# Loads in order of need in one queue, statistics of two tiles ahead of normalising, and skip terms ahead of the last back rotation, in a fused state-space and SwiGLU kernel

## The chip, the cores and the metric

The kernel runs on one core of one Trainium2 chip. Its engines run beside each other and wait for one another by semaphores: TensorE (PE in the profile, with PEld for its weight loads), VectorE (DVE), ScalarE (ACT), GpSimd (POOL) and SyncE (SP). SP, ACT and POOL also issue DMAs, each into its own queue. The metric is the device time of one execution in microseconds; a smaller one is better. The time given is the median of several executions.

## What is computed

The input x has 2048 rows of 512 values. Each row is normalised (mean and variance, no scale or shift), and two branches are added to x:

```python
xn = _layernorm(x, axis=-1)
return x + _A_ref(xn, ...) + _B_ref(xn, ...)

# A: a diagonal complex state-space layer
Lam_bar = jnp.exp(dt * Lam)
B_bar = ((Lam_bar - 1.0) / Lam)[:, None] * Bmat
Bu = jnp.einsum("bld,pd->blp", x + 0j, B_bar)
h = Lam_bar[None, :] * h + Bu[:, t, :]          # for t in range(2048)
y = 2.0 * jnp.einsum("blp,dp->bld", hseq, Cmat).real + x * Dskip[None, None, :]

# B: a SwiGLU feed-forward layer, 512 -> 1376 -> 512
return (silu(x @ w_gate) * (x @ w_up)) @ w_down
```

Types are bfloat16 in and out.

## The kernel before

**Tiling.** The 2048 rows are 16 tiles of 128 rows, in 4 chunks of 4 tiles. Normalised rows are transposed into xnT (features on partitions), so that a chunk is 512 columns. The 1376 hidden features are 11 tiles, the last of 96 features with a packing of its own.

**Stages for each chunk.** gateup_tile(c, fi) makes one hidden tile: four matmuls of 512 columns with the gate weights and four with the up weights (line 423), then SiLU and a copy on ACT (lines 437 and 438), and for two tiles together a product on DVE (line 442). bproj_tile (line 348) projects into the state space. The recurrence is made real: rotation() multiplies by cosines and sines (lines 358 to 372), DVE scans run along the 512 columns (line 390), and a second rotation turns back into wt. out_ffn (line 510) and out_ssm (line 520) add both branches into one PSUM tile for each row tile.

**The way to the output.** Chunks 0 to 2: out is first set to x by a DRAM to DRAM copy, then the results of out_ssm (copied by ACT into res, line 526) are added to it by accumulating DMAs that POOL issues (line 527). The skip term, xn times Dskip, is made by skip_op: ACT makes xn again into one of three xr buffers (line 482), DVE multiplies it into xall (line 490), and skip_store adds a whole chunk to out with one accumulating DMA on POOL (line 494). For the last chunk skip_op adds the skip term to x (lines 487 and 488), out_ssm adds the matmul result on DVE (line 523), and SP and ACT store it (line 524); the last row tile goes out in three blocks of 256, 128 and 128 columns.

**The order of the work.** PE's order is written out by hand. DVE's long work is held in a backlog of operations, each with a cost in microseconds and a tag. pump(us) is called with the PE time just issued and adds it to what is owed; operations go out while at least half of the next one's cost is owed. An operation may have a part for ACT that goes out when the operation is among the next three. need(tag) sends out the backlog up to the last operation of that tag. multiply() sends out products, which count against what is owed.

**The head (lines 599 to 660).** The first chunk's tiles come one by one. For each: statistics on DVE (ln_stats, or ln_stats_half for half the columns), ln_rstd_act (Ln and Exp on ACT), normalising on DVE (norm_dve, line 203), four transposes on PE into PSUM (xT_pe, line 215), a copy into xnT on ACT or DVE (lines 219 and 217). head_mm then does the gate and up matmuls of the first three hidden tiles for these 128 columns (line 604), into six PSUM banks that are held until all four tiles are through. There are eight banks. Ahead of the first tile, dummy() keeps PE at work on zeros (line 577).

**Loads.** They are issued at the start on SP and ACT in the order of lines 116 to 142. The gate and up weights come in groups of hidden tiles: 0 and 1, then 2, then 3 to 6, then 7 to 9. SP goes on with rows of chunk 1 and with the transposing loads of B (line 135), then weights of group 3, the rest of B and the last weights; load_late brings the others.

Of the kernel before, what the change touches and what calls it, by code (L numbers as in the profile page):

```python
# [23 lines left out]
def kernel(  # L24
# [17 lines left out]
    nc = tc.nc  # L42
    _, L, D = A_x.shape
    Pst = A_Lambda_re.shape[0]
    F = B_w_gate.shape[1]
    assert L % 512 == 0 and D % 128 == 0 and Pst % 128 == 0 and Pst == D
    CW = 512
# [26 lines left out]
    def bank(shape=(128, CW), dtype=F32):  # L74
        return psum.tile(list(shape), dtype, name="ps")
# [10 lines left out]
    xall = const.tile([128, NT, D], BF16, name="xall")  # L86
    xnT = const.tile([128, KD, L], BF16, name="xnT")

    fgroups = [(0, 2), (2, 3), (3, 7), (7, FT - 1)]
    wg_g, wu_g = [], []  # L90
    for gi, (a, b) in enumerate(fgroups):
        cols = min(F, b * 128) - a * 128
# [12 lines left out]
    def wslice(groups, fi, k):  # L105
        for (a, b), t in zip(fgroups, groups):
            if a <= fi < b:
                return t[:, k, (fi - a) * 128:(fi - a) * 128 + fsz[fi]]


    def load_w1(q, tiles, view, gi):
        a, b = fgroups[gi]
        q.dma_start(out=tiles[gi][:], in_=view[:, :, a * 128:min(F, b * 128)])


    nc.sync.dma_start(out=xall[:, 0, :], in_=x_v[:, 0, :])
    nc.vector.memset(xall[:, 1, 0:2], 0.0)
    nc.scalar.dma_start(out=xall[:, 1, :], in_=x_v[:, 1, :])
    load_w1(nc.sync, wg_g, wg_v, 0)
    load_w1(nc.scalar, wu_g, wu_v, 0)  # L120
    load_w1(nc.sync, wg_g, wg_v, 1)
    load_w1(nc.scalar, wu_g, wu_v, 1)
    nc.sync.dma_start(out=xall[:, 2, :], in_=x_v[:, 2, :])
    nc.scalar.dma_start(out=xall[:, 3, :], in_=x_v[:, 3, :])
    nc.scalar.preload_act_table_set("natural_log_exp_and_others")
    load_w1(nc.sync, wg_g, wg_v, 2)
    load_w1(nc.sync, wu_g, wu_v, 2)
    prm_rows = const.tile([128, 128], BF16, name="prm_rows")
    nc.gpsimd.memset(prm_rows[:], 0.0)
    for i, v in enumerate((A_Lambda_re, A_Lambda_im, A_log_dt)):  # L130
# [2 lines left out]
    for part, src in enumerate((A_B_re, A_B_im)):  # L133
        for k in range(KD):
            nc.sync.dma_start_transpose(out=BT[:, part, k, :], in_=src[:, k * 128:(k + 1) * 128])
        if part == 0:
            load_w1(nc.sync, wg_g, wg_v, 3)
            load_w1(nc.sync, wu_g, wu_v, 3)

    nc.sync.dma_start(out=w_last[:, :, 0:LB], in_=wg_v[:, :, FL + LA:F])  # L140
    nc.sync.dma_start(out=w_last[:, :, LB:LB + LA], in_=wg_v[:, :, FL:FL + LA])
# [40 lines left out]
    def ln_stats_half(n, h):  # L182
        nc.vector.bn_stats(out=stats[:, n, h, :], in_=xall[:, n, h * HW:(h + 1) * HW])  # L183
        if h == 1:
            nc.vector.bn_aggr(out=mv[:, n, :], in_=stats[:, n, :, :])
# [3 lines left out]
    def ln_rstd_act(n):  # L189
        nc.scalar.activation(out=lnv[:, n:n + 1], in_=mv[:, n, 1:2], func=ACT.Ln, bias=eps_t[:])  # L190
        nc.scalar.activation(out=rstd[:, n:n + 1], in_=lnv[:, n:n + 1], func=ACT.Exp, scale=-0.5)
# [9 lines left out]
    def norm_dve(n, lo=0, hi=D):  # L201
        c, i = divmod(n, TPC)
        nc.vector.tensor_scalar(out=xn_tile(c)[:, i, lo:hi], in0=xall[:, n, lo:hi], scalar1=mv[:, n, 0:1],  # L203
                                scalar2=rstd[:, n:n + 1], op0=ALU.subtract, op1=ALU.mult)
# [370 lines left out]
    def dummy(n, cols):  # L575
        for _ in range(n):
            nc.tensor.matmul(warm[:, 0:cols], lhsT=junk[:, 0:128], rhs=junk[:, 0:cols], start=True, stop=True)  # L577
# [18 lines left out]
    H = 3  # L596
    held = []

    def head_mm(fi, i, k0=0, k1=KD):
        if len(held) <= fi:  # L600
            held.append((bank(), bank()))
        for ps, groups in zip(held[fi], (wg_g, wu_g)):
            for k in range(k0, k1):
                nc.tensor.matmul(ps[:, i * 128:(i + 1) * 128], lhsT=wslice(groups, fi, k),  # L604
                                 rhs=xnT[:, k, i * 128:(i + 1) * 128], start=(k == 0), stop=(k == KD - 1))

    HK = KD // 2
    dummy(9, CW)
    ln_stats(0)
    ln_rstd_act(0)  # L610
    ln_stats_half(1, 0)
    norm_dve(0, 0, HW)
    xT_pe(0, 0, HK)
    norm_dve(0, HW, D)
    dummy(3, 128)
    xT_pe(0, HK, KD, on_dve=True)
    ln_stats_half(1, 1)
    ln_rstd_act(1)
    for fi in range(2):
        head_mm(fi, 0, 0, HK)  # L620
    for fi in range(2):
        head_mm(fi, 0, HK, KD)
    norm_dve(1)
    xT_pe(1)
    head_mm(2, 0)
    ln_stats(2)
    ln_rstd_act(2)
    ln_stats_half(3, 0)
    for fi in range(H):
        head_mm(fi, 1)  # L630
    norm_dve(2)
    xT_pe(2)
    ln_stats_half(3, 1)
    ln_rstd_act(3)
    nc.gpsimd.iota(out=jidx[:], pattern=[[1, CW]], base=0, channel_multiplier=0,
                   allow_small_or_imprecise_dtypes=True)
    pp = prm_transpose()
    for fi in range(H):
        head_mm(fi, 2)
    norm_dve(3)  # L640
    xT_pe(3, on_dve=True)
    params_a(pp)
    params_a2()
    params_sin()
# [5 lines left out]
    queue("tables", tables[2:])  # L650
    ln_nb(0, TPC)
    for fi in range(H):
        head_mm(fi, 3)
        gu_out(0, fi, *held[fi])
        pump(GU / 4)
    pump(2.0)
# [77 lines left out]
    out_chunk(0)  # L734
    gateup_chunk(2)
    bproj_chunk(3)
    queue_ssm(3)
    out_chunk(1)
    gateup_chunk(3)
    for n in range(0, NT):  # L740
        queue("skip", [skip_op(n, n >= NT - TPC)])
        if n % TPC == TPC - 1 and n < NT - TPC:
            queue("skip", [(0.0, lambda c=n // TPC: skip_store(c))])
    out_chunk(2)
    need("skip")
    out_chunk(3)
# [30 lines left out]
```

## Time and profile before

| what | value |
|---|---|
| median of 3 runs | 183.76 us (183.74 to 183.78) |
| profiled execution: its own time | 184.05 us |
| profiled execution: span | 182.3 us |
| PE busy | 173.8 us, 95% of the span |
| DVE busy | 156.1 us, 86% |
| ACT busy | 104.9 us, 58% |
| POOL busy | 23.5 us, 13% |
| granted PE clock | 1.0 throughout |
| read from and written to HBM | 8.03 MB and 5.24 MB |

The span runs from the first to the last event that the profiler records in the program; the execution's own time holds a little around it. Rows of a timeline give start and length in microseconds, engine, line of the kernel, operation, what is written and read, the number of instructions put together, and in square brackets how long the engine was idle and what released it. SPq and ACTq are the queues in which an engine issues DMAs; the time there is that of issuing, and a DMA's time to landing is given apart from it. Rows of the chain of waits give start, length, and the engine and line that held up the end. Matmul ends are modelled, so a block of matmuls carries a little time behind its last start.

### The profile page before, as it was taken

How to read it: one execution, taken by the hardware profiler on the slowest of the kernel's cores; microseconds unless marked ns; L12 is line 12 of the kernel's file. 1: busy time of each engine (PE TensorE's matmuls, PEld its weight loads, DVE VectorE, ACT ScalarE, POOL GpSimd, SP SyncE). 2: the span in 40 equal slices, each digit the busy share in tenths (PEclk: the TensorE clock that was granted, in tenths of full speed). 3: DMA queues.
4: the chain of work that ended last, by engine and by line, in shares of the span. 5: the costliest groups of instructions: out<-in, count | busy, mean ns of one | idle time of the engine just before them, and what ended most of it. 6: DMA issues, size and time to landing. Idle time of an engine off the chain costs nothing.

```text
span 182.3 us, 2494 instructions
## 1 busy us (share of the span) xinstructions
PE 173.8 (95%) x907; PEld 83.6 (46%) x923; DVE 156.1 (86%) x251; ACT 104.9 (58%) x189; POOL 23.5 (13%) x30
## 2 busy tenths in 40 slices
PE   7779999999999999999999999999999999999990
PEld 2576444444444444444444444444444444444760
DVE  3648999799999999999999999999999999766051
ACT  3329958798479959122699761024867740697000
POOL 6000300000500000014500000015000000222250
PEclk9999999999999999999999999999999999999999
DMA  6999546995034900001750000007300000097755
GB/s 163 322 273 226 87 87 164 352 185 116 1 58 86 345 4 0 0 4 28 97 107 0 0 0 4 0 0 79 36 0 5 0 0 0 0 143 119 104 101 111
DMA packets 29515, 15.53 MB, mean 85 GB/s; under 512 B 19360, under 2 KB 29440, under 8 KB 29472
## 3 DMA queue, kind: packets, MB, share of 16 engines
q1 hardware_dynamic: 24416, 11.34, 25.8%
q0 software_dynamic: 3456, 3.28, 14.2%
q10 hardware_dynamic: 1632, 0.75, 1.5%
q8 instruction: 7, 0.11, 0.3%
q14 instruction: 4, 0.03, 0.1%
HBM read 8.03 MB, written 5.24 MB: 73 GB/s over the span
## 4 chain that ended last, share of the span: by engine, by line
PE 95%; DVE 1%; ACT 1%; issue 1%
PE ps L423 35%; PE ps L510 21%; PE ps L348 15%; PE ps L520 15%; PE ps L604 2%; PE ps L577 2%; PE ps L449 2%; PE ps L459 1%; PE ps L215 1%; ACT xnT L219 1%; DVE xnT L217 0%; DVE xn L203 0%; DVE stats L183 0%; ACT lnv L190 0%; DVE xall L523 0%
## 5 line engine op out<-in xcount | busy, mean ns | idle before, releaser
L510 PE MATMUL ps<-wd_sb,guT 128*128 128x512 bf16 (+4 forms) x195 | 38.6, 355 | 0.2
L423 PE MATMUL ps<-xnT,wg 128*128 128x512 bf16 x143 | 37.6, 379 | 0.3
L423 PE MATMUL ps<-xnT,wu 128*128 128x512 bf16 x146 | 37.5, 379 | 0.1
L390 DVE TENSOR_TENSOR_SCAN g<-r_t,car,u 128x512 bf16<-128x512 f32 x24 | 28.9, 1265 | 0.0
L520 PE MATMUL ps<-CF,wt 128*128 128x512 bf16 (+2 forms) x140 | 28.1, 355 | 0.2
L348 PE MATMUL ps<-xnT,BT 128*128 128x512 bf16 x126 | 28.2, 379 | 0.1
L510 PEld LDWEIGHTS <-guT 128*128 128x128 bf16 (+1 forms) x198 | 18.5, 98 | 19.9
L437 ACT ACTIVATE guT<-ps 128x512 bf16<-128x512 f32 x40 | 25.1, 628 | 3.0 <-PE ps L423 2.9
L438 ACT CAST u<-ps 128x512 bf16<-128x512 f32 x40 | 24.7, 617 | 3.2 <-PE ps L423 3.2
L423 PEld LDWEIGHTS <-wu 128*128 128x128 bf16 x148 | 14.5, 98 | 17.4
L423 PEld LDWEIGHTS <-wg 128*128 128x128 bf16 x148 | 14.3, 98 | 17.6 <-issue 0.8
L526 ACT CAST res<-ps 128x512 bf16<-128x512 f32 x12 | 6.8, 583 | 23.5 <-PE ps L520 23.5
L520 PEld LDWEIGHTS <-wt 128*128 128x128 bf16 x144 | 13.5, 98 | 14.3
L527 POOL DMA_DIRECT2D out_dram<-res x12 | 10.6, 1040 | 72.7 <-ACT res L526 67.6
L348 PEld LDWEIGHTS <-BT 128*128 128x128 bf16 x128 | 12.5, 98 | 15.1
L350 ACT CAST u<-ps 128x512 bf16<-128x512 f32 x32 | 17.7, 613 | 2.3 <-PE ps L348 2.2
L482 ACT ACTIVATE xr<-xall,nb,rstd 128x512 bf16<-128x512 bf16 x16 | 11.6, 804 | 8.5 <-DVE xall L490 8.5
L442 DVE TENSOR_TENSOR guT<-guT,u 128x1024 bf16<-128x1024 bf16 x20 | 13.6, 682 | 0.0
L195 POOL TENSOR_TENSOR rstd<-ve,neg_half 128x4 f32<-128x4 f32 x3 | 5.3, 1751 | 45.4 <-DVE ve L194 45.4
L179 DVE BATCH_NORM_STATS2 stats<-xall 128x6 f32<-128x512 bf16 x14 | 9.4, 671 | 2.0 <-DMA xall<-in_A_x_dram 2.0
L358 DVE TENSOR_TENSOR pm<-u,c 128x2048 bf16<-128x2048 bf16 x8 | 9.8, 1221 | 1.2 <-ACT c L275 1.1
L208 ACT ACTIVATE xn<-xall,nb,rstd 128x512 bf16<-128x512 bf16 x8 | 6.5, 822 | 6.3 <-DVE nb L198 6.3
(103 smaller groups left out, 170.9 us busy)
## 6 DMA issues: line engine op xcount, KB each, us to landing
out_dram<-in_A_x_dram SPq DMA_DIRECT2D x1, 1536.0 KB, 8.9
out_dram<-res POOLq DMA_DIRECT2D x12, 128.0 KB, 3.2
out_dram<-xall POOLq DMA_DIRECT2D x3, 512.0 KB, 6.0
wd_sb<-in_B_w_down_dram SPq DMA_DIRECT2D x1, 1280.0 KB, 9.9
xall<-in_A_x_dram SPq DMA_DIRECT2D x1, 1024.0 KB, 6.7
wg<-in_B_w_gate_dram SPq DMA_DIRECT2D x1, 512.0 KB, 5.7
wu<-in_B_w_up_dram SPq DMA_DIRECT2D x1, 512.0 KB, 6.8
xall<-in_A_x_dram SPq DMA_DIRECT2D x1, 512.0 KB, 6.7
```

The costliest lines, as they stand in the source:

```text
L348: nc.tensor.matmul(ps[:], lhsT=BT[:, part, k, q * 128:(q + 1) * 128], rhs=xnT[:, k, c * CW:(c + 1) * CW], start=(k == 0), stop=(k == KD - 1))
L350: nc.scalar.copy(out=u_tiles[c][:, part, q, :], in_=ps[:])
L358: V.tensor_tensor(out=t[:], in0=flat(src()[:, i]), in1=flat(tab[:]), op=ALU.mult)
L390: V.tensor_tensor_scan(out=g()[:, part, q, :], data0=r_t[:, q:q + 1].to_broadcast([128, CW]), data1=u_tiles[c][:, part, q, :], initial=ini ...
L423: nc.tensor.matmul(ps[:fs, lo:hi], lhsT=wslice(groups, fi, k), rhs=xnT[:, k, c * CW + lo:c * CW + hi], start=(k == 0), stop=(k == KD - 1))
L437: nc.scalar.activation(out=guT[:fs, fi, :], in_=psg[:fs], func=ACT.Silu)
L438: nc.scalar.copy(out=u_pair[c][:fs, fi % 2, :], in_=psu[:fs])
L442: products.append(lambda: V.tensor_tensor(out=g, in0=g, in1=u, op=ALU.mult))
L482: nc.scalar.activation(out=box["xr"][:], in_=xall[:, n, :], func=ACT.Identity, scale=rstd[:, n:n + 1], bias=nb[:, n:n + 1])
L510: nc.tensor.matmul(o[:], lhsT=gu_tiles[c][:fsz[fi], fi, i * 128:(i + 1) * 128], rhs=wd_sb[:fsz[fi], fi, lo:hi], start=(fi == 0), stop=False)
L520: nc.tensor.matmul(o[:], lhsT=w_tiles[c][:, part, q, i * 128:(i + 1) * 128], rhs=CF[:, part, q, lo:hi], start=False, stop=(part == 1 and q ...
L527: nc.gpsimd.dma_start(out=out_v[:, n, lo:hi], in_=res[:, lo:hi], accum_op=ALU.add)
```

## The change

It has three parts.

- Loads. Hidden tiles 0 to 2 become one weight group, of 384 columns, that is loaded in two halves along the contraction (k 0 and 1, k 2 and 3), for gate and for up. All of these go through SP: rows of tile 0, gate halves, rows of tile 2, up halves, rows of tile 3, then the group of tiles 3 to 6. ACT issues the rows of tile 1 alone, and its table load follows at once.
- Head. Statistics of tile 1 are taken whole, ahead of normalising tile 0. There are ten dummies of 512 columns, not nine. Both half copies of tile 0 are on ACT. The head matmuls go by weight matrix: head_mm takes one of the two weight groups, and a list of hidden tiles, and blocks are cut so that transposes of the next tile stand between the groups of one block.
- Tail. The skip operations and stores of chunks 0 to 2 stand in the backlog between the last chunk's scans and its back rotation. They are queued ahead of out_chunk(1). The skip operations of the last chunk stay behind gateup_chunk(3).

```diff
-    fgroups = [(0, 2), (2, 3), (3, 7), (7, FT - 1)]
+    fgroups = [(0, 3), (3, 7), (7, FT - 1)]
...
+    def load_w1_half(tiles, view, gi, k0, k1):
+        a, b = fgroups[gi]
+        nc.sync.dma_start(out=tiles[gi][:, k0:k1, :], in_=view[:, k0:k1, a * 128:min(F, b * 128)])
+
     nc.sync.dma_start(out=xall[:, 0, :], in_=x_v[:, 0, :])
     nc.vector.memset(xall[:, 1, 0:2], 0.0)
     nc.scalar.dma_start(out=xall[:, 1, :], in_=x_v[:, 1, :])
-    load_w1(nc.sync, wg_g, wg_v, 0)
-    load_w1(nc.scalar, wu_g, wu_v, 0)
+    nc.scalar.preload_act_table_set("natural_log_exp_and_others")
+    load_w1_half(wg_g, wg_v, 0, 0, KD // 2)
+    load_w1_half(wg_g, wg_v, 0, KD // 2, KD)
+    nc.sync.dma_start(out=xall[:, 2, :], in_=x_v[:, 2, :])
+    load_w1_half(wu_g, wu_v, 0, 0, KD // 2)
+    load_w1_half(wu_g, wu_v, 0, KD // 2, KD)
+    nc.sync.dma_start(out=xall[:, 3, :], in_=x_v[:, 3, :])
     load_w1(nc.sync, wg_g, wg_v, 1)
-    load_w1(nc.scalar, wu_g, wu_v, 1)
-    nc.sync.dma_start(out=xall[:, 2, :], in_=x_v[:, 2, :])
-    nc.scalar.dma_start(out=xall[:, 3, :], in_=x_v[:, 3, :])
-    nc.scalar.preload_act_table_set("natural_log_exp_and_others")
-    load_w1(nc.sync, wg_g, wg_v, 2)
-    load_w1(nc.sync, wu_g, wu_v, 2)
+    load_w1(nc.sync, wu_g, wu_v, 1)
...
-    def head_mm(fi, i, k0=0, k1=KD):
-        if len(held) <= fi:
-            held.append((bank(), bank()))
-        for ps, groups in zip(held[fi], (wg_g, wu_g)):
+    def head_mm(i, groups, k0=0, k1=KD, tiles=range(H)):
+        which = 0 if groups is wg_g else 1
+        for fi in tiles:
+            if len(held) <= fi:
+                held.append((bank(), bank()))
             for k in range(k0, k1):
-                nc.tensor.matmul(ps[:, i * 128:(i + 1) * 128], lhsT=wslice(groups, fi, k),
+                nc.tensor.matmul(held[fi][which][:, i * 128:(i + 1) * 128], lhsT=wslice(groups, fi, k),
                                  rhs=xnT[:, k, i * 128:(i + 1) * 128], start=(k == 0), stop=(k == KD - 1))
 
     HK = KD // 2
-    dummy(9, CW)
+    dummy(10, CW)
     ln_stats(0)
     ln_rstd_act(0)
-    ln_stats_half(1, 0)
+    ln_stats(1)
     norm_dve(0, 0, HW)
+    norm_dve(0, HW, D)
+    ln_rstd_act(1)
     xT_pe(0, 0, HK)
-    norm_dve(0, HW, D)
     dummy(3, 128)
-    xT_pe(0, HK, KD, on_dve=True)
-    ln_stats_half(1, 1)
-    ln_rstd_act(1)
-    for fi in range(2):
-        head_mm(fi, 0, 0, HK)
-    for fi in range(2):
-        head_mm(fi, 0, HK, KD)
+    xT_pe(0, HK, KD)
     norm_dve(1)
+    head_mm(0, wg_g, 0, HK)
     xT_pe(1)
-    head_mm(2, 0)
+    head_mm(0, wu_g, 0, HK)
     ln_stats(2)
     ln_rstd_act(2)
-    ln_stats_half(3, 0)
-    for fi in range(H):
-        head_mm(fi, 1)
+    head_mm(0, wg_g, HK, KD)
+    head_mm(0, wu_g, HK, KD)
+    ln_stats(3)
     norm_dve(2)
+    ln_rstd_act(3)
+    head_mm(1, wg_g)
     xT_pe(2)
-    ln_stats_half(3, 1)
-    ln_rstd_act(3)
+    norm_dve(3)
     nc.gpsimd.iota(out=jidx[:], pattern=[[1, CW]], base=0, channel_multiplier=0,
                    allow_small_or_imprecise_dtypes=True)
+    head_mm(1, wu_g)
     pp = prm_transpose()
-    for fi in range(H):
-        head_mm(fi, 2)
-    norm_dve(3)
+    head_mm(2, wg_g)
     xT_pe(3, on_dve=True)
+    head_mm(2, wu_g)
     params_a(pp)
...
     for fi in range(H):
-        head_mm(fi, 3)
+        head_mm(3, wg_g, tiles=[fi])
+        head_mm(3, wu_g, tiles=[fi])
         gu_out(0, fi, *held[fi])
...
-    queue_ssm(3)
+    fwd3, back3 = ssm_ops(3)
+    queue("ssm3", fwd3)
+    for n in range(0, NT - TPC):
+        queue("skip", [skip_op(n, False)])
+        if n % TPC == TPC - 1:
+            queue("skip", [(0.0, lambda c=n // TPC: skip_store(c))])
+    queue("ssm3", back3)
     out_chunk(1)
     gateup_chunk(3)
-    for n in range(0, NT):
-        queue("skip", [skip_op(n, n >= NT - TPC)])
-        if n % TPC == TPC - 1 and n < NT - TPC:
-            queue("skip", [(0.0, lambda c=n // TPC: skip_store(c))])
+    for n in range(NT - TPC, NT):
+        queue("skip", [skip_op(n, True)])
     out_chunk(2)
```

The later calls of load_w1 take the new group numbers.

More of the change, by code (lines that the diff above doesn't have):

```diff
@@ L136 @@
         if part == 0:
-            load_w1(nc.sync, wg_g, wg_v, 3)
-            load_w1(nc.sync, wu_g, wu_v, 3)
+            load_w1(nc.sync, wg_g, wg_v, 2)
+            load_w1(nc.sync, wu_g, wu_v, 2)
     nc.sync.dma_start(out=w_last[:, :, 0:LB], in_=wg_v[:, :, FL + LA:F])
```

## The prediction, made before the changed kernel was run

> **What bounds the kernel now.** I read the page first: its span, and the chain of waits by engine.
>
> ```profile
> span 182.3 us, 2494 instructions
> ...
> PE 95%; DVE 1%; ACT 1%; issue 1%
> ```
>
> TensorE (PE) sets the end almost alone. Only time in which PE waits, or time before and after its work, can be won. The stage table (stretch, length, then busy time of PE, PEld, DVE, ACT, POOL, then granted clock, DMA share, GB/s) says where that is:
>
> ```profile
> 5.17:15.03 9.86, 7.58 (x117) 6.92 (x117) 5.32 (x21) 3.87 (x12) 0.00 (x0) 1.00 1.09 288
> 15.03:178.17 163.14, 162.25 (x785) 75.52 (x798) 148.53 (x223) 99.22 (x175) 20.29 (x19) 1.00 0.37 69
> ```
>
> From 15.03 us to the last matmul PE lacks 0.89 us in 163. In the head, 5.17 to 15.03, it lacks 2.28 us by busy time, and more by work: the chain of waits in order of time gives the price of a block.
>
> ```profile
> 9.06 1.50 PE ps L604 x24
> 10.56 0.24 PE ps L215 x4
> 10.80 0.02 issue
> 10.82 0.59 ACT xnT L219
> ...
> 13.22 0.43 DVE xnT L217
> 13.65 0.04 issue
> 13.69 1.50 PE ps L604 x24
> ```
>
> 24 head matmuls (L604) are one column block: 1.50 us with the 0.16 us that the last one drains, so 1.34 us of PE, 0.056 each. Four transposes (L215) cost 0.24. Four blocks and their transposes are 4 x 1.58 = 6.3 us; the stage has 9.86. So about 3.5 us of the head are waiting, and the pattern is in the rows: transposes, then a copy (0.59 on ACT, 0.43 on DVE) while PE has nothing, then 24 matmuls. The first blocks wait longer, for the statistics:
>
> ```profile
> 4.61 0.63 PE L577 MATMUL ps<-junk 128*128 128x512 bf16 x1
> 5.17 0.40 PE L215 MATMUL ps<-ident,xn 128*128 128x128 bf16 x2
> ...
> 7.99 0.40 PE L215 MATMUL ps<-ident,xn 128*128 128x128 bf16 x4 [0.91 <-DVE xn L203]
> ```
> ```profile
> 3.17 0.69 DVE L179 BATCH_NORM_STATS2 stats<-xall 128x6 f32<-128x512 bf16 x1 [1.98 <-DMA xall<-in_A_x_dram]
> ...
> 4.00 0.39 DVE L183 BATCH_NORM_STATS2 stats<-xall 128x6 f32<-128x256 bf16 x1
> 4.77 0.60 DVE L203 TENSOR_SCALAR xn<-xall,mv,rstd 128x256 bf16<-128x256 bf16 x2 [0.38 <-ACT rstd L191]
> ...
> 7.52 0.41 DVE L203 TENSOR_SCALAR xn<-xall,mv,rstd 128x512 bf16<-128x512 bf16 x1 [0.60 <-ACT rstd L191]
> ```
> ```profile
> 4.21 0.29 ACT L190 ACTIVATE lnv<-mv,eps_t 128x1 f32<-128x1 f32 x1
> ...
> 5.60 0.37 ACT L219 COPY xnT<-ps 128x256 bf16<-128x256 bf16 x1 [0.87 <-PE ps L215]
> ```
>
> Units that I take from these: statistics plus aggregation 0.83 (3.17 to 4.00); Ln to normalising 0.56 (4.21 to 4.77); normalising to transposing 0.47 (7.52 to 7.99); half a copy 0.37.
>
> **The change, part 1: the head's order.** I lay the new order out against these units.
>
> The second tile's statistics are now whole and ahead of normalising: 4.00 + 0.83 = 4.83, so normalising starts 0.06 later than its 4.77 and its first half ends at about 5.17. That is covered by the tenth dummy: the ninth starts at 4.61, eight steps from 1.23 make 0.42 each, the tenth runs from 5.03 and frees PE at 5.46. So the first transposes move from 5.17 to 5.46: **0.29 us lost**. Cost of the dummy with no cover: the same 0.29, already counted.
>
> From there, in microseconds: first half copied 5.89 to 6.26 (before, 5.60 to 5.97); the second half, formerly on DVE, now follows on ACT, 6.29 to 6.66. PE starts head matmuls at 6.32, six of gate half one, to 6.65. Meanwhile the second tile's reciprocal root is done (Ln at 4.93, normalising at 5.49 to 5.90), so its four transposes run at 6.65 with no wait: the 0.91 us is gone. Its copy runs 7.06 to 7.65 behind the two half copies. PE has the three other half groups of block 0 for that: 18 x 0.056 = 1.01, from 6.87 to 7.88. Cover is whole.
>
> Block 1's gate part (12 matmuls, 0.67) runs 7.88 to 8.55. Late next is tile 2: its Ln stands behind the copy on ACT (7.65), so normalising starts at 8.21, transposing at 8.68: 0.13 wait. Its copy ends at 9.69; block 1's up part and the parameter transpose fill PE to 9.63: 0.11 wait. Block 2's gate part to 10.41, tile 3's transposes to 10.63 (normalised by 9.15), its copy on DVE 10.83 to 11.25 under block 2's up part to 11.30. Block 3 follows to 12.64. The row that tells where it ended before:
>
> ```profile
> 15.03 1.03 PE L423 MATMUL ps<-xnT,wg 128*128 128x512 bf16 x3
> ```
>
> 15.03 - 12.64 = 2.39, so **2.4 us gained, net of the dummy**. Bounds: if only the 0.91 wait goes and the 0.29 is paid, 0.6; if no wait is left at all, 3.5 - 0.3 - about 0.8 of the first copy that nothing can cover = 2.4 to 2.7. I take 2.4, the laid-out chain, since every piece of it is a measured duration.
>
> Given back later? ACT's chain into the first SiLU hangs on the third copy (13.22), as does block 3 (13.69), so both move alike and the PSUM distance between ACT and PE stays. DVE's work list, too, starts at that copy.
>
> **Part 2: loads.** ACT loses three issues, SP gains them. Bytes do not change; row lengths do (rows of 256 and 512 bytes become 768).
>
> ```profile
> 2.00:6.00 4.00, 4.00 (x15) 1.63 (x14) 1.79 (x5) 2.15 (x4) 2.09 (x6) 1.00 1.05 270
> 31.00:34.00 3.00, 3.00 (x15) 1.37 (x14) 1.84 (x3) 1.28 (x3) 0.00 (x0) 1.00 1.00 337
> ```
> ```profile
> 1.20 0.97 SPq L113 DMA_DIRECT2D wg<-in_B_w_gate_dram  x2
> ...
> 3.57 0.51 SPq L113 DMA_DIRECT2D wu<-in_B_w_up_dram  x1
> ...
> 6.07 5.87 SPq L135 DMA_TRANSPOSE BT<-in_A_B_re_dram  x4
> ```
> ```profile
> wu<-in_B_w_up_dram SPq DMA_DIRECT2D x1, 512.0 KB, 6.8
> ```
>
> DMA moves 270 GB/s from 2 to 6 us, and 337 at 31 to 34 us, where SP's queue alone is loading. So one queue is enough. Ahead of the last half of the first up weights stand 1152 KB, 1.18 MB: 2 + 1.18/0.27 = 6.4, with landing 6.7 or so. PE wants it at 7.54: 0.8 to spare. The halves before it land at about 4, 4.7 and 5.9, needed at 6.3, 7.2 and 6.9. Tile 2 lands near 5.2, tile 3 near 7, used at 5.9 and 6.85, the latter maybe 0.2 late on DVE, which then still waits for ACT at 8.2. The group for feature tiles 3 to 6 landed at 3.57 + 6.8 = 10.4 with the same bytes ahead; it is wanted at 12.6 (gate) and 13.5 (up). Cost of the part: **nothing**, hidden by the head's PE work; its price with no cover is a rival below.
>
> SP's later work: an issue takes 0.49, so ten of them reach the first B transpose at 1.20 + 9 x 0.5 = 5.7, not after 6.07. The transposes and all that stands behind them come no later, though PE comes 2.4 us sooner:
>
> ```profile
> 13.16 6.17 SPq L135 DMA_TRANSPOSE BT<-in_A_B_im_dram  x4
> ```
> ```profile
> BT<-in_A_B_im_dram SPq DMA_TRANSPOSE x4, 3.6
> ```
> ```profile
> 22.10 4.10 PE ps L348 x19
> ```
>
> The imaginary part is issued by 19.33 and landed by about 22; its first product comes four groups of 0.86 after 22.10, at 25.5, and would be at 23.1. One us of room.
>
> **Part 3: skip terms ahead of the last back rotation.** I walked the planner: PE time is added to what is owed, an operation goes out when half its cost is owed. The twelve skip operations now go out from tile 8 of chunk 3's gate/up to the second output block, the back rotation after them.
>
> ```profile
> 144.59 2.46 DVE L390 TENSOR_TENSOR_SCAN g<-r_t,car,u 128x512 bf16<-128x512 f32 x2
> ...
> 145.70 2.23 ACT L482 ACTIVATE xr<-xall,nb,rstd 128x512 bf16<-128x512 bf16 x3
> ...
> 154.86 1.22 DVE L372 TENSOR_TENSOR wt<-pm 128x2048 bf16<-128x2048 bf16 x1
> 156.01 1.09 DVE L490 TENSOR_TENSOR xall<-xr,dsk_bc 128x512 bf16<-128x512 bf16 x3
> ```
> ```profile
> 171.02 7.11 PE L520 MATMUL ps<-CF,wt 128*128 128x512 bf16 x47
> ```
>
> On the times of before, DVE reaches the skips at about 147.6. They are paced by ACT (2.23 for three, 0.74 each; three buffers, with chunk 3's last SiLU queued among them), so the last ends near 156.4 and the back rotation near 163.7, instead of 156.08. Who waits: the output matmuls of chunk 3 at 171.02, 7 us later. The last gate/up products come at 154.6, wanted at 161.4. So on PE this is **nothing**, with 7 us of cover. The third store leaves POOL near 156.5 instead of at 168.26, and that is the tail:
>
> ```profile
> 168.26 1.30 POOL L494 DMA_DIRECT2D out_dram<-xall  x1 [2.98 <-DMA out_dram<-res]
> 174.63 2.66 POOL L527 DMA_DIRECT2D out_dram<-res  x3 [5.07 <-DMA out_dram<-xall]
> ```
> ```profile
> out_dram<-xall SPq DMA_DIRECT2D x1, 128.0 KB, 1.8
> ```
> ```profile
> out_dram<-xall SPq DMA_DIRECT2D x1, 32.0 KB, 2.7
> ```
>
> Three accumulating stores wait for the last skip store and then run on top of the final ones. The final store on SP, 32 KB, takes 2.7 us; the first of the 128 KB ones, ahead of POOL's three, took 1.8. With POOL's stores done by about 168, the last landing comes 2.7 - 1.8 = 0.9 sooner at most, 0 at least (a fixed landing time). I take **0.8**, near the row of the quiet queue. The Trainium skill (DMA: Bandwidth & Descriptors, Anatomy of one DMA) gives a fixed cost of about 2.0 us for a DMA, mostly the receipt of the last byte; by that the tail would win 0.7 and not 0.8. The 1.8 row is a little below it.
>
> **Sum.** The profiled execution took 184.05 us, 1.75 of it outside its span. 184.05 - 2.4 - 0.8 = 180.85; the median of the runs, 183.76, is 0.29 below that execution, so **180.6 us**.
>
> **The rivals.**
>
> The tail stays: the final stores take 2.7 us anyway, or POOL's stores are still late because the skips come later than I walked. Against it, the 1.8 row. Time: 183.76 - 2.4 = 181.4.
>
> The head gives half: ACT now does all three first copies and four roots in one order, and each round may again be as long as its chain of copy, Ln, normalising, transposing (0.59 + 0.56 + 0.47 = 1.6, with the copy after it 2.2, against 1.58 of PE work). For it, the waits of 0.13 and 0.11 that I already find; if each of three rounds shows 0.4 more, 1.2 of the 2.4 are lost: 181.8, and 182.6 without the tail.
>
> Slower, by the single queue: if SP's queue alone brought half the 270 GB/s, 135, the 2.36 MB to the end of the up group of tiles 3 to 6 would land at 2 + 17.5 = 19.5, wanted at 13.5: 6 us lost, 186.6. It turns slower than before where that landing passes 13.5 + 3.2 = 16.7, below 160 GB/s. Against it, 337 at 31 us. The Trainium skill (DMA: Bandwidth & Descriptors, Bandwidth) asks for DMAs of 1 MiB and more, which speaks against halves of 192 KB. Of the rows here, 270 GB/s was reached with loads of 128 to 512 KB in flight together, so the trace does not bear a loss out.
>
> No change: the skip work on ACT holds up chunk 3's last SiLU until PE has no bank, and eats the 3.2 us: 183.8. From the walk, six banks are free for the four output blocks, so ACT may be some 7 us late before it counts.
>
> **How the numbers follow.** Forecast 180.6 (180.0 to 181.1): 0.66. Tail stays, 181.4: 0.13. Head half, 181.8 to 182.6: 0.12. No change, 183.8: 0.04. Slower, 186.6: 0.05. A measurement of this kernel can tell about 0.2%, 0.37 us, from no change. Faster: 0.66 + 0.13 + 0.12 = 0.91; same 0.04; slower 0.05. The range 179.9 to 182.0 holds the first two cases and half of the third, 0.85; its low end is a head of 2.7 with a tail of 0.9 and 0.3 for what I cost too high.
>
> **What would show it.** Right: the first L423 matmul at 12.4 to 12.9 us; no wait for a normalised second tile; waits in the head under 0.2 each; the three out_dram<-res stores of chunk 2 ended before 170; final store of 32 KB under 2.1 us; back rotation ended some 7 us before its reader. Wrong: PE waiting for weights in the head, a gap between 12 and 20 us that was not there, or output matmuls of chunk 3 waiting for wt.

## The result, and the profile after

The changed kernel takes 181.06 us (median of 4 runs, 180.66 to 181.34), the kernel before 183.77 us beside it (4 runs, 183.74 to 183.87). The ratio is 0.985, with a 95% interval of 0.983 to 0.9871: faster by 1.5%. Forecast were 180.6 us and a range of 179.9 to 182.0.

The profiled execution of the changed kernel took 181.21 us with a span of 179.4 us. Lines have moved down by four or five: L427, L524, L609 and L219 are what L423, L520, L604 and L215 were. I read the same views as before. First the page: the span, and the chain of waits by engine.

```profile
span 179.4 us, 2491 instructions
...
PE 93%; DMA 2%; SPq 1%; DVE 1%; issue 1%
```

PE still sets the end, but 2% of the chain is now a DMA and 1% SP's queue. Neither was in that list before. The stage table (stretch, length, busy time of PE, PEld, DVE, ACT and POOL, granted clock, DMA share, GB/s) shows where the time came from:

```profile
5.17:13.28 8.11, 7.18 (x118) 6.56 (x116) 4.34 (x17) 3.88 (x12) 0.00 (x0) 1.00 1.19 286
13.28:176.42 163.14, 162.26 (x785) 75.42 (x798) 148.00 (x222) 98.81 (x175) 20.23 (x19) 1.00 0.40 75
```

The head ends at 13.28 instead of 15.03. From there to the last DVE add it is 163.14 us, as before to the hundredth. After that add 179.4 - 176.42 = 2.98 us are left, where 182.3 - 178.17 = 4.13 were. So the head gave 1.75, the middle nothing and the tail 1.15; 2.4 and 0.8 were forecast.

What ends last in the head now? The chain of waits in order of time (start, length, what) says it:

```profile
3.68 4.33 DMA xall<-in_A_x_dram
...
8.04 0.70 DVE stats L183
...
8.95 0.31 DVE xn L207
...
9.31 0.40 PE ps L219 x4
```

Read it from the bottom. The transposes at 9.31 are those of tile 2. They wait for tile 2 to be normalised (xn), and that stands on DVE behind the statistics of tile 3, which wait for a load that landed at 8.02. The timelines of DVE and PE show the same from both sides:

```profile
6.27 0.69 DVE L183 BATCH_NORM_STATS2 stats<-xall 128x6 f32<-128x512 bf16 x1 [0.52 <-DMA xall<-in_A_x_dram]
...
8.04 0.69 DVE L183 BATCH_NORM_STATS2 stats<-xall 128x6 f32<-128x512 bf16 x1 [0.86 <-DMA xall<-in_A_x_dram]
```

```profile
9.31 0.40 PE L219 MATMUL ps<-ident,xn 128*128 128x128 bf16 x4 [0.63 <-DVE xn L207]
...
13.28 0.38 PE L427 MATMUL ps<-xnT,wg 128*128 128x512 bf16 x1
```

DVE has 0.86 us with nothing to do, because it takes its work in order and the next item's data is not there. PE pays 0.63 of it.

### The profile page after: what moved, and what is told of

Same layout as the page of the kernel before. It is cut to its first block, busy times and chain, and to the rows that moved or that the text cites. A ratio compares the mean times of both kernels' runs of the same rounds, so it can differ in the third digit from the quotient of the medians.

```text
span 179.4 us, 2491 instructions
## 1 busy us (share of the span) xinstructions
PE 173.4 (97%) x908; PEld 83.4 (46%) x924; DVE 155.0 (86%) x248; ACT 104.8 (58%) x190; POOL 23.4 (13%) x30
## 4 chain that ended last, share of the span: by engine, by line
PE 93%; DMA 2%; SPq 1%; DVE 1%; issue 1%
PE ps L427 36%; PE ps L514 21%; PE ps L352 15%; PE ps L524 15%; DMA xall<-in_A_x_dram 2%; PE ps L609 2%; PE ps L453 2%; PE ps L463 1%; SPq L118 1%; DVE stats L183 0%; PE ps L219 0%; SPq L126 0%; SPq L120 0%; DVE xn L207 0%; DVE xall L527 0%
## 5 line engine op out<-in xcount | busy, mean ns | idle before, releaser
L427 PE MATMUL ps<-xnT,wg 128*128 128x512 bf16 x143 | 37.6, 379 | 0.3
L427 PE MATMUL ps<-xnT,wu 128*128 128x512 bf16 x146 | 37.5, 379 | 0.1
L524 PE MATMUL ps<-CF,wt 128*128 128x512 bf16 (+2 forms) x140 | 28.1, 355 | 0.2
L427 PEld LDWEIGHTS <-wu 128*128 128x128 bf16 x148 | 14.5, 98 | 17.5
L427 PEld LDWEIGHTS <-wg 128*128 128x128 bf16 x148 | 14.3, 98 | 17.6 <-issue 0.8
L524 PEld LDWEIGHTS <-wt 128*128 128x128 bf16 x144 | 13.4, 98 | 14.3
L183 DVE BATCH_NORM_STATS2 stats<-xall 128x6 f32<-128x512 bf16 x16 | 10.7, 671 | 3.2 <-DMA xall<-in_A_x_dram 3.2
L527 DVE TENSOR_TENSOR xall<-ps,xall 128x512 bf16<-128x512 f32 (+2 forms) x6 | 3.1, 514 | 9.1 <-PE ps L524 9.1
```

What stands on the lines that cost most here:

```text
L183: nc.vector.bn_stats(out=stats[:, n, 0, :], in_=xall[:, n, :])
L427: nc.tensor.matmul(ps[:fs, lo:hi], lhsT=wslice(groups, fi, k), rhs=xnT[:, k, c * CW + lo:c * CW + hi], start=(k == 0), stop=(k == KD - 1))
L524: nc.tensor.matmul(o[:], lhsT=w_tiles[c][:, part, q, i * 128:(i + 1) * 128], rhs=CF[:, part, q, lo:hi], start=False, stop=(part == 1 and q ...
```

## The experiments

The theory after this profile: the two parts add, the tail's gain comes from POOL's accumulating stores, and the head misses its forecast by the late landing of loads, made worse by DVE's order. Its rivals: the parts overlap or hide one another; the tenth dummy is what costs; two queues would land the loads sooner; whatever the head wins is given back later. In the table, "head" is the start of the first matmul of 512 columns, "middle" the time from there to the last DVE add, "rest" the span less the start of that add. Medians stand beside runs of the kernel before on the same chip (183.77 in the first batch, 183.83 for e1 to e4, 184.11 for e6 to e9, 184.09 for e10 to e12), and ratios are against these. They are taken over all runs, so they differ by up to 0.002 from the quotient of the medians. Head, middle and rest are of one profiled execution each.

| kernel | median, us | ratio, 95% interval | head | middle | rest |
|---|---|---|---|---|---|
| before | 183.77 | 1 | 15.03 | 163.14 | 4.13 |
| changed | 181.06 | 0.985 (0.983 to 0.9871) | 13.28 | 163.14 | 2.98 |
| e9: changed, once more | 180.73 | 0.9819 (0.9789 to 0.9849) | 12.80 | 163.14 | 3.06 |
| e1: head alone | 181.98 | 0.9892 (0.9877 to 0.9907) | 12.74 | 163.14 | 4.52 |
| e2: tail alone | 182.75 | 0.9931 (0.9917 to 0.9945) | 14.76 | 163.13 | 2.71 |
| e3: tile 2 first on DVE | 181.37 | 0.9863 (0.9847 to 0.9879) | 13.47 | 163.44 | 2.99 |
| e4: nine dummies | 181.05 | 0.9848 (0.9832 to 0.9863) | 13.02 | 163.14 | 3.04 |
| e6: up halves on ACT | 181.81 | 0.9859 (0.9835 to 0.9884) | 13.67 | 163.14 | 3.19 |
| e7: no up load | 181.07 | 0.9834 (0.9807 to 0.9861) | 12.31 | 163.46 | 3.33 |
| e8: e6 and e3's order | 181.5 | 0.985 (0.9824 to 0.9877) | 13.58 | 163.14 | 3.18 |
| e10: tiles on ACT | 181.0 | 0.9826 (0.9803 to 0.985) | 12.92 | 163.14 | 3.24 |
| e11: e10 and another order | 180.92 | 0.9824 (0.9801 to 0.9847) | 13.07 | 163.14 | 3.19 |
| e12: more DVE work | 182.14 | 0.9891 (0.9867 to 0.9915) | 12.60 | 164.45 | 2.95 |

The rest varies from 2.71 to 3.33 us among the kernels with early skip terms, though their final store takes 1.4 to 1.5 us in every one of these profiles. What else lies in it no run shows, so differences of 0.3 us in the rest of a single profile are not read as gains.

### e1 and e2: each part alone

e1 puts the skip terms back, so it has the new loads and head alone:

```diff
-    fwd3, back3 = ssm_ops(3)
-    queue("ssm3", fwd3)
-    for n in range(0, NT - TPC):
...
-    queue("ssm3", back3)
+    queue_ssm(3)
...
-    for n in range(NT - TPC, NT):
-        queue("skip", [skip_op(n, True)])
+    for n in range(0, NT):
+        queue("skip", [skip_op(n, n >= NT - TPC)])
...
```

> The changed kernel with the skip operations and their stores put back behind the last chunk's gate/up, as in the kernel before: loads and head alone. Theory: the head gives 1.75 us (first 512-column matmul at 13.28 instead of 15.03) and the tail nothing, so 183.77 - 1.75 = 182.0, and the final 32 KB store takes 2.7 us again, under POOL's three late stores. Rival: the tail's gain comes from the shift of the head itself, which would let POOL's stores end sooner in any case; then about 181.1 and a final store of 1.4 us.

e2 is the kernel before with that block as the change has it:

```diff
-    queue_ssm(3)
+    fwd3, back3 = ssm_ops(3)
+    queue("ssm3", fwd3)
+    for n in range(0, NT - TPC):
...
+    queue("ssm3", back3)
```

> The kernel before with the skip operations and stores of chunks 0 to 2 put ahead of the last back rotation, nothing else. Theory: the end moves from 3.84 us behind the last DVE addition to 2.7, so 183.77 - 1.1 = 182.65; PE's head ends at 15.03 as before; the final 32 KB store takes 1.4 us. Rival: 183.8, if the order of the skips alone does nothing.

The head alone gives 183.83 - 181.98 = 1.85 us, the tail alone 1.08. Together 2.93, against 2.71 for both in the first batch: they add, within the spread of the runs. (e1's head is 2.29 sooner in its profile and its rest 0.39 longer than before; that makes the 1.9 of its span. So the 182.0 expected from a head of 1.75 and an unchanged rest was met partly by luck.) The rows of the tail tell why. POOL's timeline first, then the issues of DMAs with their median time to landing; of e1, with the skip terms late:

```profile
165.87 1.30 POOL L498 DMA_DIRECT2D out_dram<-xall  x1 [2.94 <-DMA out_dram<-res]
172.33 2.66 POOL L531 DMA_DIRECT2D out_dram<-res  x3 [5.16 <-DMA out_dram<-xall]
```
```profile
out_dram<-xall SPq DMA_DIRECT2D x1, 32.0 KB, 2.9
```

and of e2, with the skip terms early:

```profile
165.25 2.63 POOL L527 DMA_DIRECT2D out_dram<-res  x3 [1.82 <-ACT res L526]
```
```profile
out_dram<-xall SPq DMA_DIRECT2D x1, 32.0 KB, 1.4
```

The same 32 KB store takes 2.9 us where three accumulating stores were issued 3.6 us ahead of the last add, and 1.4 us where they were issued 12.6 us ahead. The releaser in brackets has changed too: in e1 POOL waits 5.16 us for the skip store ahead of these three, in e2 only 1.82 us for ACT's copy. In e2 the wait for the skip store is still there (5.38 us), but it comes one store earlier, at 162.54 us, and no longer brings the three stores on top of the last ones.

### e3: normalising tile 2 ahead of the statistics of tile 3

This takes the late load out of the chain, by DVE's order alone.

```diff
-    ln_stats(3)
     norm_dve(2)
-    ln_rstd_act(3)
+    ln_stats(3)
     head_mm(1, wg_g)
     xT_pe(2)
+    ln_rstd_act(3)
     norm_dve(3)
```

> The changed kernel with tile 2 normalised ahead of tile 3's statistics on DVE, and tile 3's Ln and Exp behind tile 2's copy on ACT. Theory (tile 3's landing at 8.02 us, behind which normalising tile 2 stands on DVE, holds the head): tile 2 is normalised from 7.8 and not 8.87, its transposes start when PE is free at 8.5 and not at 9.31, tile 3 then waits some 0.3 for its own chain behind the copy, and block 3 starts near 11.5 instead of 11.95: 0.45 faster, 180.6. Rival (the chain copy, Ln, normalising on ACT holds the head): no change, 181.1.

It gained nothing: 181.37 us, of which 0.30 lies in the middle (see e7). DVE no longer waits for tile 3 ahead of tile 2, and in place of that wait stands another. PE's timeline:

```profile
7.60 0.51 PE L609 MATMUL ps<-xnT,wu 128*128 128x128 bf16 x6 [0.85 <-DMA wu<-in_B_w_up_dram]
...
9.28 0.39 PE L219 MATMUL ps<-ident,xn 128*128 128x128 bf16 x4
```

The first half of the up weights landed so late in this execution that PE waited 0.85 us for it, and tile 2 was transposed at 9.28 all the same. So the order on DVE is not the cause by itself; two loads are late together, and either is enough. What this order gives when the up half is on time, no run shows.

### e4: nine dummies instead of ten

```diff
-    dummy(10, CW)
+    dummy(9, CW)
```

> The changed kernel with nine dummies and not ten. Theory (tile 3's landing holds the head): PE's first transposes may start 0.2 sooner, but tile 2's transposes still start near 9.3 and block 3 near 11.95: no change, 181.1 within 0.2. Rival (the dummy costs what it delays): 0.2 to 0.3 faster, 180.8. A second rival: PE comes to full speed later for want of work, and the first head matmuls take 0.1 each: slower by 0.2 or more.

181.05 against 181.06 us: no difference. The first transposes start at 4.98 rather than 5.25, but PE then waits 0.52 for the up half. In that execution the dummy's time lies under the loads, and the medians show no cost of it. The changed kernel with nine dummies was not profiled in an execution whose loads were on time.

### e6 and e8: the up halves in ACT's queue

```diff
-    def load_w1_half(tiles, view, gi, k0, k1):
+    def load_w1_half(tiles, view, gi, k0, k1, q=nc.sync):
...
     nc.scalar.dma_start(out=xall[:, 1, :], in_=x_v[:, 1, :])
+    load_w1_half(wu_g, wu_v, 0, 0, KD // 2, nc.scalar)
+    load_w1_half(wu_g, wu_v, 0, KD // 2, KD, nc.scalar)
...
-    load_w1_half(wu_g, wu_v, 0, 0, KD // 2)
-    load_w1_half(wu_g, wu_v, 0, KD // 2, KD)
```

> The changed kernel with the two halves of the first up weights issued on ACT's queue, ahead of its table load, and not on SP's; all else as in the changed kernel. The stage tables show 269 GB/s from 2 to 8 us with nearly all loads in SP's queue and 291 in the kernel before with two queues. Theory (one queue leaves gaps between its loads): near 290 GB/s again, tile 3 lands at 7.4 or sooner and not at 8.0, the up half before PE wants it, and the head ends 0.4 to 0.6 sooner: 180.5. Rival (the loads are held by the memory's rate, whatever the queue): tile 3 at 8.0, 181.1.

Not faster: 181.81 us, against 180.73 for the changed kernel on the same chip (e9); the two intervals overlap. The rate from 2 to 8 us does not tell them apart. It is 295 GB/s here and 269 in the first profile of the changed kernel, but e9 and e12, with the changed kernel's queues, have 292 and 257. The up halves came earlier; but what was needed next came later. Stage row, issue row and DVE's timeline of e6:

```profile
2.00:8.00 6.00, 6.00 (x46) 3.59 (x45) 2.90 (x8) 3.61 (x8) 2.07 (x5) 1.00 0.95 295
```
```profile
xall<-in_A_x_dram SPq DMA_DIRECT2D x1, 128.0 KB, 5.4
```
```profile
7.63 0.69 DVE L183 BATCH_NORM_STATS2 stats<-xall 128x6 f32<-128x512 bf16 x1 [1.65 <-DMA xall<-in_A_x_dram]
```

Tile 2 was issued at 2.17 us in both kernels. It took 5.4 us to land here and 4.1 in the changed kernel (3.8 in e9). What differs is that the up halves, issued on ACT from 1.32 on, were in flight beside it; that they are the cause is argued from the order of issue. e8 has the same queues with e3's order on DVE and tile 2's copy on DVE (`xT_pe(2, on_dve=True)`).

> The up halves on ACT's queue as above, and besides tile 2 normalised ahead of tile 3's statistics, tile 2's copy on VectorE, tile 3's Ln and Exp behind tile 2's copy in the program. Theory (loads hold the head, and with them earlier the order on VectorE is next): another 0.2 to 0.4 below the kernel with the up halves on ACT's queue alone, 180.2. Rival: no difference from it.

It gives 181.5 us, and tile 2 takes 5.3 us to land again, with its statistics at 7.53. Two queues are no faster here: in both kernels the tile that was wanted first landed later.

### e7: the up halves not loaded at all

This one leaves out the load of 384 KB of up weights for hidden tiles 0 to 2, and uses a constant in their place. It tells how much the head could win if loads were early.

```diff
-    load_w1_half(wu_g, wu_v, 0, 0, KD // 2)
-    load_w1_half(wu_g, wu_v, 0, KD // 2, KD)
...
     nc.vector.memset(eps_t[:], EPS)
+    nc.vector.memset(wu_g[0][:], 0.01)
```

> The changed kernel without the loads of the up weights of hidden tiles 0 to 2: a constant written by VectorE in its idle time at 1.2 to 2 us stands in for these 384 KB, so that part of the input is left out. Theory (the landing of the loads holds the head): tile 3 lands near 6.7, PE waits for no weights, and the head runs as laid out in the prediction, block 3 from 11.3 and not 11.95 or, with the first tile's lead of 0.2 to 0.3, from 11.0: 0.7 to 1.0 faster, 180.2. Rival (the chain of copy, Ln and normalising holds it): 181.1.

The head has no wait for a load and ends at 12.31, 0.97 us sooner. The time is 181.07 us all the same, and the middle is 163.46: 0.32 of the 0.97 us is given back. Another 0.35 is given back in the rest (3.33), which no run explains. PE's timeline of e7 has the place of the 0.32. Blocks of four matmuls start 0.86 us apart; here it is 1.18:

```profile
88.53 1.03 PE L426 MATMUL ps<-xnT,wu 128*128 128x512 bf16 x4
89.71 1.02 PE L426 MATMUL ps<-xnT,wg 128*128 128x512 bf16 x4 [0.16 <-ACT guT L440]
```

PE finds the PSUM bank still held. ACT's SiLU that frees it stands behind normalising on ACT, and that waits for DVE. ACT's timeline of e7, and of the changed kernel:

```profile
85.61 0.81 ACT L211 ACTIVATE xn<-xall,nb,rstd 128x512 bf16<-128x512 bf16 x1 [3.21 <-DVE nb L201]
...
89.07 0.60 ACT L440 ACTIVATE guT<-ps 128x512 bf16<-128x512 f32 x1
```
```profile
86.14 0.81 ACT L212 ACTIVATE xn<-xall,nb,rstd 128x512 bf16<-128x512 bf16 x1 [2.76 <-DVE nb L202]
...
89.59 0.60 ACT L441 ACTIVATE guT<-ps 128x512 bf16<-128x512 f32 x1
```

PE is 0.97 sooner in e7, but ACT only 0.53, since DVE is. Where did DVE lose the other 0.44? Its timelines of e7 and of the changed kernel part near 28 us:

```profile
27.32 0.69 DVE L271 TENSOR_SCALAR pm<-pm 128x1024 f32<-128x1024 f32 x1
28.52 0.69 DVE L273 TENSOR_SCALAR pm<-pm 128x1024 f32<-128x1024 f32 x1 [0.51 <-ACT s L278]
```
```profile
28.27 0.69 DVE L272 TENSOR_SCALAR pm<-pm 128x1024 f32<-128x1024 f32 x1
29.07 0.69 DVE L274 TENSOR_SCALAR pm<-pm 128x1024 f32<-128x1024 f32 x1
```

1.20 from start to start in e7, 0.80 in the changed kernel: 0.40 lost there, and kept for 57 us. e3's rows are the same (28.47 and 29.66), and its middle is 163.44. The changed kernel's PE takes the bank at 90.36, 0.77 behind the SiLU's start; e7's took it as soon as it could, 0.64 behind. So at this place DVE may fall behind PE by 0.13 us and no more: 0.40 to 0.44 less 0.13 is 0.27 to 0.31, and 0.32 was lost.

### e9: the changed kernel once more

> The changed kernel once more, unaltered, beside the three above on the same chip. All theories: 181.1, and a spread of some 0.5 us between its runs, several times that of the kernel before. Theory (the landing of the loads holds the head): its own trace shows a start of tile 2's transposes that follows the landing of tile 3 or of the up half, by 1.3 or by 0.9 us.

180.73 us (5 runs, 180.61 to 181.58), and another head. Its DVE and PE timelines:

```profile
7.46 0.70 DVE L183 BATCH_NORM_STATS2 stats<-xall 128x6 f32<-128x512 bf16 x1 [0.57 <-DMA xall<-in_A_x_dram]
```
```profile
8.82 0.40 PE L219 MATMUL ps<-ident,xn 128*128 128x128 bf16 x4
...
12.80 1.03 PE L427 MATMUL ps<-xnT,wg 128*128 128x512 bf16 x3
```

The same program, but tile 3 was there 0.56 us earlier and PE did not wait for tile 2. The head ended at 12.80, 0.48 sooner. What holds it now? The chain of waits of e9 goes through PE alone, from the dummies on:

```profile
1.23 4.45 PE ps L581 x10
5.67 0.21 PE ps L219 x2
...
7.27 1.68 PE ps L609 x30
8.94 0.28 PE ps L219 x4
```

So no load holds the head in this execution, and e1 and e11 have the same chain there; e12's holds no load either. The distance of 1.3 us from tile 3 to tile 2's transposes that was expected is there (7.46 to 8.82), but PE's own work ended only then too, so it does not show that the load held them; in e1 the distance is 1.53 (7.23 to 8.76). "The landing of the loads holds the head" is true of some executions and not of others.

The 9 runs of this kernel lie from 180.61 to 181.58. Not all of that need be loads: the 9 of the kernel before beside e9 lie from 183.64 to 184.83.

### e10 and e11: tiles 2 and 3 in ACT's queue

```diff
     nc.scalar.dma_start(out=xall[:, 1, :], in_=x_v[:, 1, :])
+    nc.scalar.dma_start(out=xall[:, 2, :], in_=x_v[:, 2, :])
+    nc.scalar.dma_start(out=xall[:, 3, :], in_=x_v[:, 3, :])
...
-    nc.sync.dma_start(out=xall[:, 2, :], in_=x_v[:, 2, :])
...
-    nc.sync.dma_start(out=xall[:, 3, :], in_=x_v[:, 3, :])
```

> The changed kernel with the rows of tiles 2 and 3 issued on ACT's queue behind those of tile 1, ahead of the table load; the weights stay on SP in the same order. Theory (the head follows the landing of what it needs next, whichever queue brings it): tiles 2 and 3 land near 4.5 and 5.5, so DVE no longer waits for them; the up halves land no sooner than now (6.8 to 7.6 and later), so PE waits there by 0.2 to 0.5; the head ends near 12.6 in place of 12.8 to 13.3: 0.3 faster, 180.6. Rival (the chain of copy, Ln, normalising): 180.9, no change.

DVE no longer waits for tile 2 or tile 3, and PE waits for the weights instead. The row is from e10's waits (total, times, longest):

```profile
PE ps L609 <- DMA wu<-in_B_w_up_dram: 0.7, 1, 0.7
```

181.0 us, as the changed kernel. e11 also moves both up halves of block 0 later on PE, so that they are wanted later (`head_mm(0, wu_g, 0, HK)` behind the gate part of block 0, `head_mm(0, wu_g, HK, KD)` behind that of block 1).

> As the kernel with the tiles on ACT's queue, and PE's order fitted to the landing: both gate halves of block 0, then its first up half, then block 1's gate part, and only then block 0's last up half. Theory: no wait for weights is left, the head ends near 12.4; of the 0.5 to 0.8 that gives, what exceeds DVE's room near 90 us comes back as a wait there, unless DVE's work shifts with the head: 180.4. Rival: as the kernel without the new order, 180.6 to 180.9.

180.92 us. PE waits for no load, but the head still ends at 13.07. In this execution the first six head matmuls took longer, 0.1 us each and not 0.056, as PE's timelines of e11 and of the changed kernel show:

```profile
6.35 0.80 PE L609 MATMUL ps<-xnT,wg 128*128 128x128 bf16 x6
```
```profile
5.99 0.50 PE L609 MATMUL ps<-xnT,wg 128*128 128x128 bf16 x6 [0.18 <-ACT xnT L223]
```

Neither is told from the changed kernel by its time.

### e12: a little more work on DVE behind the head

This asks whether DVE has room, now that PE comes sooner: four memsets of a scratch tile right behind the head's last small operations.

```diff
     ln_nb(0, TPC)
+    for _ in range(4):
+        nc.vector.memset(junk[:], 0.0)
```

> The changed kernel with four writes of the zero tile, 0.27 us each, put on VectorE behind the head's parameters and ahead of the statistics of chunk 1: about 1.0 us of VectorE work, none of PE's. Theory (by the traces VectorE has about 0.1 us to spare before ACT's normalising of chunk 2 holds up a SiLU and PE runs out of banks near 90 us): 0.8 to 0.9 slower, 181.8. Rival (VectorE is 2 to 7 us ahead of its readers everywhere, as at chunk 3): no change, 180.9.

```profile
12.98 1.45 DVE L655 MEMSET junk<- 128x256 uint32 x4
```

1.45 us of DVE work make the kernel 1.1 us slower than e10 on the same chip and 1.2 slower than e11, though the head ends at 12.60. The middle is 164.45, 1.31 longer: the 1.45 less the 0.13 of room that e7 gave. The four writes took 1.45 us where 1.0 had been reckoned. PE's waits in e12 name two places that the changed kernel does not have, at 33.4 and at 91.0 us:

```profile
PE ps L352 <- ACT u L354: 0.7, 1, 0.7
PE ps L427 <- ACT guT L441: 0.2, 1, 0.2
```

So DVE has next to no slack behind the head, though it is busy only 148.00 of 163.14 us and PE never waits for it there by name. The slack of 0.13 us is that of one place, near 90 us; DVE holds up ACT, and ACT holds PE's banks.

## Why the prediction was right, and where it was off

The time came within 0.5 us of the forecast partly by luck: the head gave 0.65 us less than forecast, the tail 0.35 more, and the two misses cancel in part.

**What bounds the kernel.** Right. Only PE's waits in the head and the time behind its last matmul could be won, and only there was anything won: the middle is 163.14 us before and after.

**The head's order.** Right in its working. Laid out were transposes of tile 2 at 8.68 and the head's end 3.96 later, at 12.64. Measured is a distance of 3.97 in the changed kernel (9.31 to 13.28) and 3.98 in e9 (8.82 to 12.80); everything behind tile 2 went as laid out. The step that was off is the landing of loads ahead of it. "Tile 3 near 7, ... maybe 0.2 late on DVE" was costed at nothing, and the issue rows of the changed kernel say otherwise:

```profile
3.68 0.47 SPq L129 DMA_DIRECT2D xall<-in_A_x_dram  x1
```
```profile
xall<-in_A_x_dram SPq DMA_DIRECT2D x1, 128.0 KB, 4.3
```

3.68 + 4.33 (the chain's figure for the same load) = 8.0. The rate was not wrong: 269 GB/s from 2 to 8 us, where 270 was assumed.

```profile
2.00:8.00 6.00, 5.69 (x47) 3.30 (x46) 3.41 (x9) 3.22 (x10) 2.08 (x5) 1.00 0.95 269
```

Tile 3 and all ahead of it are 1.31 MB, moved by 2 + 1.31/0.27 = 6.85 us if nothing else were moved meanwhile. It landed 1.2 us after that, where I allowed little over 0.1. What lies in the 1.2 us (bytes of the loads queued behind, or the report of the landing) no run separates. The first up half was too early in the forecast as well: put at 5.9, it landed at 6.8 in the changed kernel and was waited for until 6.96 in e4 and 7.60 in e3.

In e9 tile 3 was taken up at 7.46, and the transposes came 0.14 later than laid out. That 0.14 is no load: PE's first six head matmuls took 0.09 each and not 0.056 (6.35 to 6.88). So the loads, costed at nothing, cost 0.6 us in one execution and nothing in another: 12.74 (e1), 12.80 (e9) and 13.28 are three heads of one and the same code, for 12.64 forecast. The first transposes, laid out at 5.46 with the tenth dummy, started at 5.25 in the changed kernel and at 5.47 in e9. What the dummy costs stays open: in e4 a load hid it, and in e9 the chain runs on from it on PE.

**SP's later work.** "Come no later" was wrong. The four transposes of B's imaginary part were issued from 15.02 to 20.11 us in the changed kernel, from 13.16 to 19.33 before. The room that was reckoned covered it: PE has no wait on them.

**Given back later.** The text said that ACT's chain, PE and DVE's list all hang on the same copy and move alike. They do: 163.14 in the changed kernel and in e9, e1, e4, e6, e8, e10 and e11, for heads from 12.74 to 13.67. e7, e3 and e12 show where it ends: when DVE alone is held up by more than about 0.13 us. "Move alike" was right and has no more room than that.

**Skip terms and tail.** Right, with 1.15 us for 0.8. POOL issues the third skip store from 154.38 (forecast near 156.5 on the times of before, which is 154.75 less the 1.75 us of the head) and the last accumulating stores from 163.74. The final store takes 1.4 us, as the issue row of the changed kernel has it:

```profile
154.38 1.28 POOL L498 DMA_DIRECT2D out_dram<-xall  x1 [1.56 <-DVE xall L494]
...
163.74 2.63 POOL L531 DMA_DIRECT2D out_dram<-res  x3 [2.03 <-ACT res L530]
```
```profile
out_dram<-xall SPq DMA_DIRECT2D x1, 32.0 KB, 1.4
```

The bound of 0.9 at most was too low: it took the 1.8 us of a 128 KB store for one of 32 KB. The Trainium skill (DMA: Bandwidth & Descriptors, Anatomy of one DMA) gives about 2.0 us as the fixed cost of a DMA, in a section on DMAs that GpSimd issues. The whole store that SP issued here took 1.4 us. The measurement decides, and the 0.7 us that the prediction worked out from the page was too low.

**The back rotation.** Right. On DVE and PE:

```profile
160.11 1.22 DVE L376 TENSOR_TENSOR wt<-pm 128x2048 bf16<-128x2048 bf16 x1
```
```profile
169.27 5.89 PE L524 MATMUL ps<-CF,wt 128*128 128x512 bf16 x28
```

It ends at 161.3, 8 us ahead of its reader. Forecast was 163.7 on the times of before, which is 161.95 less the 1.75 us of the head.

**The rivals.** The tail stays: refuted by e2, 1.08 us for the tail alone. The head gives half: not as told, by ACT's chain of copies, but a loss of up to 0.6 us from loads is there in some executions. Slower by the single queue: refuted at its price; SP's queue and ACT's one tile brought 269 GB/s, and e6 with two queues is not faster. Its kind was right in part: a wait for a load ends last in the head in the profiles of the changed kernel, e3 and e4, and in none of e1, e9 and e12, which have the same loads. The skip work on ACT eats the gain: refuted, the middle is unchanged.

**What stays open.** Why DVE stops for 0.5 us near 28 us in e3 and e7. The profile names ACT's sine, but in the changed kernel the same DVE instruction starts at 29.07 with no such wait, while the sine there, by ACT's timeline, still runs to 29.33:

```profile
28.27 1.06 ACT L279 ACTIVATE s<-pm 128x1024 bf16<-128x1024 f32 x1
```

Open, too, is what lies in the 1.2 us between bytes moved and landing, why it differs between executions, and what lies in the rest besides the last store. None of these was tried further.

## What to carry to other kernels

Before moving a stage forward, lay out its new order with durations from the trace, and give each load a landing time with an uncertainty of its own: bytes ahead of it divided by the rate was up to 1.2 us too early here, and two loads wanted at the same moment make it useless to mend the one alone. Put loads that are all wanted soon in order of need; with the up halves in a second queue, the tile that was wanted first took 5.4 and 5.3 us to land and not 3.7 to 4.1 (e1, e9 and the changed kernel). Profile the same kernel more than once before calling what bounds it: the same head ended on a load in one profile and on PE's own work in another. Accumulating stores that run on top of the last store lengthen it, so bring them out early where the engine that waits has room.

## What was not expected of the hardware

- The landing of a load in a full queue varies between executions of one program. Tile 3, issued at 3.68 us, was taken up by DVE at 8.04 in one and 7.46 in another. Which of the other runs had late loads, only profiles would tell.
- A 32 KB store took 1.4 us with no accumulating store in flight beside it and 2.9 us on top of three of them (e2 and e1), twice as long.
- The ten dummies did not take the same time. PE's timelines of the changed kernel, e9 and e10:

```profile
1.23 4.19 PE L581 MATMUL ps<-junk 128*128 128x512 bf16 x10 [1.23 <-DVE eps_t L164]
```
```profile
1.23 4.45 PE L581 MATMUL ps<-junk 128*128 128x512 bf16 x10 [1.23 <-DVE eps_t L164]
```
```profile
1.23 3.70 PE L581 MATMUL ps<-junk 128*128 128x512 bf16 x10 [1.23 <-DVE eps_t L164]
```

4.19, 4.45 and 3.70 us for the same ten instructions from the same start. In the timelines they start 0.43 us apart at first and 0.21 apart later. PE goes over to the faster step at about 4.1 us in e10 and at the tenth dummy, 5.0, in the changed kernel. In e9 and e11 all ten go at the slow step, and the first six head matmuls, at 6.35 us, are still slow: 0.09 and 0.1 us each and not 0.056. So the moment lies between 4.1 and nearly 7 us. The granted clock reads 1.00 over the dummies and does not show it. The Trainium skill (TensorE: Matmul & The Clock Gate, Part 1) says that the clock is raised by a window that runs on its own and does not start with the kernel, so that the moment varies by 0.5 us either way. That it varies agrees with the traces; here it varies by more than 2 us. In the changed kernel and in e10 the earlier start did not decide the time, since a load ended last; in e9 and e11, where none did, the later one is in the head.
